# Kept output products of six of eight steps in high and low parts, four operand sets, and half of layer two's weight sums by accumulating DMAs

## The chip, the cores and the metric

One Trainium2 chip, one of its cores. The time is the device time of one execution in microseconds (us); of several runs the median counts.

## What is computed

```python
qn = q / (np.linalg.norm(q, axis=1, keepdims=True) + 1e-06)
kn = k / (np.linalg.norm(k, axis=1, keepdims=True) + 1e-06)
s = kn.transpose(0, 2, 1) @ qn / tau              # 256 x 256
a = softmax(s, -1)                                # over 6016 tokens: v @ a
x = (v @ a).reshape(6016, 256)
h = x @ w_in;  x = (h * sigmoid(1.702 * h)) @ w_out       # 256 -> 2048 -> 256
h = x @ w2_in; x = np.maximum(0.01 * h, h) @ w2_out       # 256 -> 2048 -> 256
```

All arrays are float32, but the four weights, which come as 64-bit floats and are put together from their words on the chip.

## The kernel before

**Stages.** Up to about 50 us q and k are read and the attention matrix is made. Then come two layers over six token pairs each, twelve pairs in all, numbered 0 to 11 (`steps`): pairs 0 to 5 are layer one, 6 to 11 layer two. A pair is 2 x 512 tokens, the sixth pair of each layer (5 and 11) 2 x 448. A pair runs eight steps f, each with 2 x 128 hidden features. Pair 0 is the front stage (`hidden_first`), which goes on to about 146 us beside the making of the weights. Pairs 1 to 3 run `step`, which uses Strassen's scheme with seven products for the first matrix of the layer and the plain way for the second. Pairs 4 to 11 (`FIRST` = 4) run `strassen_step`, with seven products for the first matrix and seven for the second; the last two steps of pair 11 are of the other kind.

**Number format.** A product a * b is taken as three float32r matmuls, high * high, low * high and high * low (`terms`, L100). The high part is a cast (`halves`, `cast`, ACT or DVE), the low part a DVE subtraction behind it (`subtract`, through L107).

**Kept products.** The seventh output product of a step is not run in the step. Its right side, g21, is kept for all eight steps (`retained`), and the products run at the end of the pair in two bursts (`burst`, L1340), in the first step of the next pair: steps 4, 5, 0, 1 at the hook "burst", steps 2, 3, 6, 7 at the hook "join". The steps in `SPLIT` (2 to 5) are kept in high and low parts and run as three float32r matmuls, the ones in `RAW` (0, 1, 6, 7) as one float32 matmul. The high part is copied in the step, the low part is subtracted in `first_stage`, which runs near the start of step f+1.

**Operand sets.** `operands` hands out pairs of tiles in turn, three calls a step (g0, g1, g2), from five sets: four in the space of the first layer's output weights, the fifth in the two buffers with the tag "gs".

**Weights.** Layer one's sums are made by `sums_first`: `combine` sums four blocks of a weight in place by four DVE instructions, casts and lows follow, and the stores to DRAM. In the front stage `go_on(n)` runs the generator `jobs` for n yields, with the casts on DVE; what is left by then is done one piece a step, with the casts on ACT. Then `words_of` makes layer two's sixteen pieces, one a step in pairs 1 to 3: `bits` puts a piece together in a tile `ta` (two buffers), a cast of the base blocks, `second` (their low parts, the store, the sums by `combine`), a cast of the sums ("rest", L406, ACT), and `third` (their low parts and the store). Casts run in `run_casts`, in the middle of the step, `close` runs what is in `closing` behind the cast of g22, `run_due` what is in `due` at the step's end, and then `begin_next` starts a piece. The sign of the sums of w2_in is turned in some places (`minus_sum`, L113), since the second layer's input blocks are made by accumulating DMAs of GpSimd's queue (L1487), which can add but not subtract.

**What sets the order.** Each engine runs its instructions in the order in which the code is written (`manual_schedule`), and waits where data or a buffer is not there.

Of the kernel before, what the change touches and what calls it, by code (L numbers as in the profile page):

```python
# [17 lines left out]
def tile_kernel(  # L18
# [61 lines left out]
    x2 = [dram.tile([P, 4, w], F32, name=f"x2{p}") for p, w in enumerate(width)]  # L80
    raw1 = [dram.tile([P, 2, 4, P], F32, name=f"raw1{f}") for f in range(NF)]
    w2a = [dram.tile([P, 7, 2, P], F32, name=f"w2a{f}") for f in range(NF)]
    w2o = [dram.tile([P, 8, 2, P], F32, name=f"w2o{f}") for f in range(NF)]
    SPLIT = (2, 3, 4, 5)
    RAW = (0, 1, 6, 7)
    w2r = dram.tile([P, len(RAW), P], F32, name="w2r")
# [40 lines left out]
    with tc.manual_schedule():  # L127
# [28 lines left out]
        def load_piece(key):  # L156
            name, f = key
            if name == "both":
                t = raws[key] = early.tile([P, 2, 4, P], F32, tag="cv", name="cb", bufs=3)
                nc.sync.dma_start(out=t, in_=raw1[f])  # L160
                return
# [35 lines left out]

        def combine(a, turned=False):

            (minus_sum if turned else add)(a[:, 2], a[:, 3], a[:, 2])  # L200
            yield
            subtract(a[:, 3], a[:, 0], a[:, 3])
            yield
            if turned:
                minus_sum(a[:, 0], a[:, 2], a[:, 0])
            else:
                subtract(a[:, 0], a[:, 2], a[:, 0])
            yield
            subtract(a[:, 1], a[:, 1], a[:, 0])
            yield  # L210
# [48 lines left out]
        def convert(key):  # L259

            name, f = key
            if key not in scaled:
                scale_words(raws[key])
                scaled.add(key)
            yield from bits(key)
            scale_next()
            yield
            a = words_out.pop(key)
            flat = a.rearrange("p k c -> p (k c)")
            if name == "wo":  # L270
                hi, lo = (wo[f][:, s].rearrange("p k c -> p (k c)") for s in range(2))
                for j in range(2):
                    nc.sync.dma_start(
                        out=raw1[f][:, 1, 0::3] if j == 0 else raw1[f][:, 1, 1:3],
                        in_=a[:, 2 * j:2 * j + 2],
                    )
                nc.vector.tensor_copy(hi, flat)
                yield
                subtract(lo, flat, hi.bitcast(F32))
                yield  # L280
                return
            if name == "wi":
                wi = early.tile([P, 2, BLK], F32R, tag="ws", name="wi", bufs=2)
                (nc.scalar.copy if f == 0 else nc.vector.tensor_copy)(wi[:, 0], flat)
                yield
                subtract(wi[:, 1], flat, wi[:, 0].bitcast(F32))
                ready[f] = wi
                yield
                return
# [13 lines left out]
        def sums_first(f):  # L303
# [9 lines left out]

            yield from combine(t[:, 0])
            high(lambda: wa[f][:, 3:, 0], t[:, 0])
            yield from combine(t[:, 1])
            high(out_blocks, t[:, 1])

            def second():
                subtract(wa[f][:, 3:, 1], t[:, 0], wa[f][:, 3:, 0].bitcast(F32))  # L320
# [3 lines left out]
                subtract(x[:, :, 1], t[:, 1], x[:, :, 0].bitcast(F32))  # L324
                nc.sync.dma_start(out=w1o[f][:, 2:6], in_=x.bitcast(F32))
# [14 lines left out]
        def words_of(key):  # L340
# [30 lines left out]

            if name == "w2i":
                def both_bases():
                    x = kept["x"] = new_blocks(name)
                    nc.scalar.copy(x[:, 0, 0], a[:, 0])
                    nc.scalar.activation(
                        out=x[:, 1:3, 0], in_=a[:, 1:3], func=AF.Copy, scale=-1.0
                    )
                casts.append(both_bases)
            else:  # L380
                high(base_blocks, a[:, some])

            def second():
                x = kept["x"]
                if name == "w2i":
                    subtract(x[:, 0, 1], a[:, 0], x[:, 0, 0].bitcast(F32))
                    minus_sum(x[:, 1:3, 1], a[:, 1:3], x[:, 1:3, 0].bitcast(F32))
                else:
                    subtract(x[:, some, 1], a[:, some], x[:, some, 0].bitcast(F32))
                if name == "w2i":  # L390
                    nc.sync.dma_start(out=dst[:, :3], in_=x[:, :3].bitcast(F32))
                else:
# [7 lines left out]
                    else:  # L400
                        raw = early.tile([P, P], F32, tag="wr", name="wr")
                        nc.vector.tensor_copy(raw, a[:, 1])
                        nc.sync.dma_start(out=w2r[:, RAW.index(f)], in_=raw)
                for _ in combine(a, name == "w2i"):
                    pass
                casts.insert(0, lambda: nc.scalar.copy(rest_blocks(), a))  # L406
                closing.append(third)

# [7 lines left out]

            due.append(second)

# [359 lines left out]
        fold_half(raw0, 0, 1)  # L778
        nc.sync.dma_start(out=raw1[0][:, 0], in_=raw0)
        folded.add(0)  # L780
# [5 lines left out]
        def fold(f):  # L786
# [10 lines left out]
            subtract(lo, raw, hi.bitcast(F32))  # L797
            nc.sync.dma_start(out=raw1[f][:, 0], in_=raw)
            folded.add(f)
# [374 lines left out]

        sets = [(4 - 3 * (NF * (LAST - FIRST) + REST - 1)) % 5]

        def operands(name):
            i = sets[0] % 5
            sets[0] += 1
            if i == 4:  # L1180
                return [late.tile([P, 2, BLK], F32R, tag="gs", name=name, bufs=2) for _ in range(2)]
            return [
                (early if n < EARLY else late).tile([P, 2, BLK], F32R, tag=f"wo{n}", name=name)
                for n in (2 * i, 2 * i + 1)
            ]
# [3 lines left out]
        def retained(i, f):  # L1189
# [13 lines left out]
            elif n > 1:  # L1203
                t = late.tile([P, 2, BLK], F32R, tag=("cc", "gq")[n - 2], name="keep1")
                keep[i, f] = t[:, :, :w]
# [11 lines left out]
        def strassen_step(i, f):  # L1217
# [51 lines left out]
            def first_stage():  # L1269
# [47 lines left out]
        def begin_drain(i):  # L1317
# [40 lines left out]
            def part_two():  # L1358
                if i == LAST:
                    return  # L1360
                add(to["c"], to["c"], sums[i, M5])
                add(tb, ta, sums[i, M7])

            def join():
                burst(other)
                if i == LAST:
                    add(ta, ta, sums[i, M6])
                    add(tb, ta, sums[i, M7])
                    add(ta, ta, sums[i, M5])
# [62 lines left out]
        def place_v(i, n):  # L1432
            nc.vector.transpose(out=staged_x[i][:, n], in_=vblocks_in.pop(n))

        def cast(to, i, n, j):
            nc.scalar.copy(to[:, 0, n, :width[i % NPAIR]], staged_x[i][:, j])

        def low(to, i, n, j):
            w = width[i % NPAIR]
            subtract(to[:, 1, n, :w], staged_x[i][:, j], to[:, 0, n, :w].bitcast(F32))  # L1440

# [218 lines left out]
```

## Time and profile before

| | us |
|---|---|
| median of 3 runs (1005.89 to 1007.33) | 1006.01 |
| profiled execution | 1006.63 |
| its span, first to last instruction | 1004.9 |
| PE busy | 997.7 (99%) |
| DVE busy | 881.5 (88%) |
| ACT busy | 760.8 (76%) |
| GpSimd (POOL) busy | 21.8 (2%) |

PE is TensorE's matmuls, DVE VectorE, ACT ScalarE, SP the queue of most DMAs. Matmuls are pipelined: a record of 512 columns lasts about 0.39 us, but the next one starts 0.23 us after it. So what a matmul takes on PE is read from one start to the next. A row of a timeline joins neighbours of the same kind; its time runs to the end of the last record.

### The profile page before, as it was taken

How to read it: one execution, taken by the hardware profiler on the slowest of the kernel's cores; microseconds unless marked ns; L12 is line 12 of the kernel's file. 1: busy time of each engine (PE TensorE's matmuls, PEld its weight loads, DVE VectorE, ACT ScalarE, POOL GpSimd, SP SyncE). 2: the span in 40 equal slices, each digit the busy share in tenths (PEclk: the TensorE clock that was granted, in tenths of full speed). 3: DMA queues.
4: the chain of work that ended last, by engine and by line, in shares of the span. 5: the costliest groups of instructions: out<-in, count | busy, mean ns of one | idle time of the engine just before them, and what ended most of it. 6: DMA issues, size and time to landing. Idle time of an engine off the chain costs nothing.

```text
span 1004.9 us, 13108 instructions
## 1 busy us (share of the span) xinstructions
PE 997.7 (99%) x4448; PEld 824.6 (82%) x4448; DVE 881.5 (88%) x1304; ACT 760.8 (76%) x1221; POOL 21.8 (2%) x31
## 2 busy tenths in 40 slices
PE   9999999999999999999999999999999999999998
PEld 8888887887888888877998887887887887788897
DVE  7899977878887887999898998998998998998986
ACT  7775557787878787886887886886886897797683
POOL 0000000000000000000000000000000000000000
PEclk9999999999999999999999999999999999999999
DMA  9866477745546753764976775875875875785662
GB/s 347 271 178 183 153 236 247 249 174 189 158 152 195 228 177 84 255 211 139 308 242 218 263 227 168 240 237 180 248 225 193 219 234 188 211 260 178 177 205 48
DMA packets 161619, 208.36 MB, mean 207 GB/s; under 512 B 100624, under 2 KB 126736, under 8 KB 160400
## 3 DMA queue, kind: packets, MB, share of 16 engines
q1 hardware_dynamic: 153808, 200.38, 61.4%
q0 software_dynamic: 3456, 6.16, 3.7%
q10 hardware_dynamic: 4288, 0.98, 0.5%
q8 instruction: 35, 0.57, 0.2%
q14 instruction: 32, 0.26, 0.1%
HBM read 161.87 MB, written 45.61 MB: 206 GB/s over the span
## 4 chain that ended last, share of the span: by engine, by line
PE 97%; DMA 1%; DVE 1%; issue 0%; ACT 0%; ACTq 0%; SPq 0%; DVEq 0%
PE h L100 53%; PE y L841 18%; PE y L100 17%; PE y L1340 5%; PE y L565 3%; DMA qk<-in_k_dram 1%; PE h L712 1%; PE h L841 0%; PE y L712 0%; DVE cc L107 0%; ACTq L498 0%; PE y L670 0%; DVE ta L107 0%; PE h L585 0%; DVE ta L247 0%
## 5 line engine op out<-in xcount | busy, mean ns | idle before, releaser
L100 PE MATMUL h<-xa,wi 128*128 128x512 f32 (+1 forms) x765 | 201.9, 385 | 0.0
L100 PE MATMUL y<-g,wo 128*128 128x512 f32 (+1 forms) x744 | 198.5, 389 | 0.4 <-issue 0.4
L100 PEld LDWEIGHTS h<-xa,wi 128*128 128x128 f32 x765 | 141.5, 188 | 29.7 <-ACT tv L1233 3.3
L100 PEld LDWEIGHTS y<-g,wo 128*128 128x128 f32 x744 | 139.6, 188 | 29.2 <-issue 4.5
L100 PE MATMUL h<-xb,wi 128*128 128x512 f32 (+1 forms) x573 | 152.8, 391 | 0.0
L107 DVE TENSOR_TENSOR g<-t,g 128x1024 fp32r<-128x1024 f32 (+1 forms) x124 | 147.4, 1189 | 0.0
L100 PEld LDWEIGHTS h<-xb,wi 128*128 128x128 f32 x573 | 106.9, 188 | 24.5 <-issue 3.2
L841 PE MATMUL y<-gd,wo 128*128 128x512 f32 (+1 forms) x498 | 124.2, 388 | 0.0
L841 PEld LDWEIGHTS y<-gd,wo 128*128 128x128 f32 x498 | 93.1, 188 | 18.7
L100 PE MATMUL h<-xa,wa 128*128 128x512 f32 x384 | 104.2, 390 | 0.1
L100 PE MATMUL h<-g,wo 128*128 128x512 f32 (+1 forms) x372 | 102.7, 384 | 0.0
L811 ACT ACTIVATE g<-g 128x512 f32<-128x512 f32 (+1 forms) x92 | 57.8, 628 | 44.3 <-DVE g L107 43.3
L100 PE MATMUL h<-xb,wa 128*128 128x512 f32 x312 | 83.9, 391 | 0.7 <-DVE xb L104 0.5
L100 PEld LDWEIGHTS h<-xa,wa 128*128 128x128 f32 x384 | 71.5, 188 | 15.4 <-DVE cc L107 0.5
L100 PEld LDWEIGHTS h<-g,wo 128*128 128x128 f32 x372 | 69.8, 188 | 12.7
L841 PE MATMUL y<-g,wo 128*128 128x512 f32 (+1 forms) x297 | 79.1, 388 | 0.0
L1277 ACT CAST g<-t 128x1024 fp32r<-128x1024 f32 (+1 forms) x62 | 63.8, 1029 | 19.5 <-DVE t L107 18.3
L107 DVE TENSOR_TENSOR g<-g,g 128x1024 fp32r<-128x1024 f32 (+1 forms) x62 | 73.9, 1192 | 0.3
L107 DVE TENSOR_TENSOR t<-g 128x1024 f32<-128x1024 f32 (+1 forms) x62 | 73.2, 1181 | 0.0
L100 PEld LDWEIGHTS h<-xb,wa 128*128 128x128 f32 x312 | 58.3, 188 | 14.0 <-DVE xb L104 1.0
L107 DVE TENSOR_TENSOR g<-tt,h 128x512 f32<-128x512 f32 (+1 forms) x62 | 41.7, 672 | 31.2 <-ACT tt L1241 26.9
L1248 ACT CAST g<-g 128x1024 fp32r<-128x1024 f32 (+1 forms) x62 | 63.7, 1027 | 2.0
(192 smaller groups left out, 1525.6 us busy)
## 6 DMA issues: line engine op xcount, KB each, us to landing
wi<-w2a SPq DMA_DIRECT2D x48, 896.0 KB, 5.5
wo<-w2o SPq DMA_DIRECT2D x46, 768.0 KB, 4.2
wi<-w1a SPq DMA_DIRECT2D x16, 896.0 KB, 6.3
wo<-w1o SPq DMA_DIRECT2D x16, 768.0 KB, 4.8
cv<-in_moe_w_in_dram SPq DMA_DIRECT2D x32, 256.0 KB, 3.4
w1a<-wa SPq DMA_DIRECT2D x8, 896.0 KB, 3.6
stg<-x SPq DMA_DIRECT2D x5, 1024.0 KB, 4.8
stg<-x POOLq DMA_DIRECT2D x20, 256.0 KB, 4.3
```

Of the source, the lines that this page charges most:

```text
L100: nc.tensor.matmul(dst, lhsT=w, rhs=x, start=start, stop=stop, skip_group_check=more)
L107: nc.vector.tensor_tensor(out=out, in0=in0, in1=in1, op=op)
L565: nc.tensor.matmul(s_ps[h][:, :C], lhsT=t[:, 1, r, h * P:(h + 1) * P], rhs=t[:, 0, r, :], start=(j == 0 and r == 0), stop=(j == last and r ...
L712: nc.tensor.matmul(pw, lhsT=e[:, d, c0], rhs=wi[:, x, d], start=i == 0, stop=i == len(todo) - 1)
L811: nc.scalar.activation(out=out, in_=in_, func=AF.Prelu, alpha=0.01)
L841: nc.tensor.matmul(ys[key][kc], lhsT=ws[x], rhs=y, start=first and n == 0, stop=closing or (final and n == 2), skip_group_check=closing,)
L1248: nc.scalar.copy(g0[0], g[:, 0::2])
L1277: nc.scalar.copy(g1[0], t13)
L1340: nc.tensor.matmul(sums[i, M1], lhsT=x, rhs=y, start=False, stop=True, skip_group_check=True,)
```

## The change

The six steps 2 to 7 are kept in parts (`SPLIT`), 0 and 1 raw; the tiles for 6 and 7 are the "gs" buffers, which the fifth operand set had. Four sets are left. In `combine` both matrices of a layer-one piece are summed at once (the DRAM tile raw1 is laid out anew for that). Of layer two's four sums two stay on DVE, and two become accumulating DMAs that GpSimd issues; `second` moves to `closing` and `third` to `due`. Signs that were turned in the weights of w2_in move to the second layer's input blocks (`turned`) and to the sums of g in layer two.

```diff
-    SPLIT = (2, 3, 4, 5)
-    RAW = (0, 1, 6, 7)
+    SPLIT = (2, 3, 4, 5, 6, 7)
+    RAW = (0, 1)
...
-            yield from combine(t[:, 0])
-            high(lambda: wa[f][:, 3:, 0], t[:, 0])
-            yield from combine(t[:, 1])
-            high(out_blocks, t[:, 1])
+            yield from combine(t)
+            high(lambda: wa[f][:, 3:, 0], t[:, :, 0])
+            high(out_blocks, t[:, :, 1])
...
-                for _ in combine(a, name == "w2i"):
-                    pass
-                casts.insert(0, lambda: nc.scalar.copy(rest_blocks(), a))
-                closing.append(third)
+                minus_sum(a[:, 2], a[:, 3], a[:, 2])
+                subtract(a[:, 3], a[:, 0], a[:, 3])
+                for to, n in ((0, 2), (1, 0)):
+                    nc.gpsimd.dma_start(out=a[:, to], in_=a[:, n], accum_op=ALU.add)
+                casts.insert(0, rest)
+
+            def rest():
+                nc.scalar.copy(rest_blocks(), a)
+                due.append(third)
...
-            due.append(second)
+            closing.append(second)
...
-        sets = [(4 - 3 * (NF * (LAST - FIRST) + REST - 1)) % 5]
+        sets = [0]
...
-            i = sets[0] % 5
+            i = sets[0] % 4
             sets[0] += 1
-            if i == 4:
-                return [late.tile([P, 2, BLK], F32R, tag="gs", name=name, bufs=2) for _ in range(2)]
...
-                t = late.tile([P, 2, BLK], F32R, tag=("cc", "gq")[n - 2], name="keep1")
+                tag = ("cc", "gq", "gs", "gs")[n - 2]
+                t = late.tile(
+                    [P, 2, BLK], F32R, tag=tag, name="keep1", bufs=2 if tag == "gs" else 1
+                )
...
-                subtract(t13, g[:, 1:3], g[:, 0:2])
-                nc.scalar.copy(g1[0], t13)
-                subtract(t24[:, 0], g[:, 2], t13[:, 0])
-                subtract(t24[:, 1], g21, t24[:, 0])
+                if layer == 1:
...
+                else:
+                    subtract(t13, g[:, 0:2], g[:, 1:3])
+                    nc.scalar.copy(g1[0], t13)
+                    minus_sum(t24[:, 0], t13[:, 0], g[:, 2])
+                    add(t24[:, 1], g21, t24[:, 0])
...
+        def turned(to, i, n):
+            return i >= NPAIR and (n in (B21, T4) if to is xbt else n == T2)
+
         def cast(to, i, n, j):
-            nc.scalar.copy(to[:, 0, n, :width[i % NPAIR]], staged_x[i][:, j])
+            hi, raw = to[:, 0, n, :width[i % NPAIR]], staged_x[i][:, j]
+            if turned(to, i, n):
+                nc.scalar.activation(out=hi, in_=raw, func=AF.Copy, scale=-1.0)
+            else:
+                nc.scalar.copy(hi, raw)
```

**PE, the second burst of pair 4's drain.** y is the sum in PSUM, keep the kept right sides, a_1 the weights. Before:

```order
L100 MATMUL h_4343<-xb,wi_4229 128x448 x3
L100 MATMUL y_3848<-g_4376,wo_4231 128x512 x2
L100 MATMUL y_3848<-g_4377,wo_4231 128x512
L1340 MATMUL y_3794<-keep_3931,a_1_3985 128x512 x6
L1340 MATMUL y_3794<-keep,a_1_3985 128x512 x2
L100 MATMUL h_4344<-xb,wi_4229 128x448 x3
```

And now:

```order
L100 MATMUL h_4298<-xb,wi_4177 128x448 x3
L100 MATMUL y_3798<-g_4332,wo_4179 128x512 x2
L100 MATMUL y_3798<-g_4333,wo_4179 128x512
L1335 MATMUL y_3744<-keep_3881,a_1_3935 128x512 x6
L1335 MATMUL y_3744<-keep_4208,a_1_3935 128x512 x3
L1335 MATMUL y_3744<-keep_4289,a_1_3935 128x512 x3
L100 MATMUL h_4299<-xb,wi_4177 128x448 x3
```

The two raw matmuls, steps 6 and 7, are now three and three.

**DVE, a step of pair 2 with a weight piece.** ta is the piece, w2i, w2o, w2is and w2os are tiles with high and low parts, cc and g those of the step's own work. Before:

```order
L107 TENSOR_TENSOR tt<-tt,h_2408 128x512
L107 TENSOR_TENSOR g_2451<-tp,g_2451 128x512
L107 TENSOR_TENSOR w2os<-ta,w2os 128x4x128
L107 TENSOR_TENSOR cc<-tv,h_2408 128x512
L107 TENSOR_TENSOR g_2452<-tt,g_2452 128x512
L107 TENSOR_TENSOR w2i<-ta,w2i 128x128
L113 SCALAR_TENSOR_TENSOR w2i<-ta,w2i 128x2x128
L113 SCALAR_TENSOR_TENSOR ta<-ta 128x128
L107 TENSOR_TENSOR ta<-ta 128x128
L113 SCALAR_TENSOR_TENSOR ta<-ta 128x128
L107 TENSOR_TENSOR ta<-ta 128x128
L242 TENSOR_SCALAR ta<-cv 128x512
```

And now, the step beside it:

```order
L107 TENSOR_TENSOR tt<-tt,h_2313 128x512
L107 TENSOR_TENSOR g_2359<-tp,g_2359 128x512
L107 TENSOR_TENSOR w2o<-ta,w2o 128x3x128
L113 SCALAR_TENSOR_TENSOR ta<-ta 128x128
L107 TENSOR_TENSOR ta<-ta 128x128
L107 TENSOR_TENSOR cc<-tv,h_2313 128x512
L107 TENSOR_TENSOR g_2360<-tt,g_2360 128x512
L107 TENSOR_TENSOR w2is<-ta,w2is 128x4x128
L903 STREAM_TRANSPOSE stg<-xr 128x512
L239 TENSOR_SCALAR ta<-cv 128x512
```

Two sums (ta<-ta) are gone from DVE; the low part of the base and the two sums that are left stand ahead of cc, and the low part of the rest, of the piece before, behind g.

**DVE, the front stage.** cb are layer one's pieces, wa and wt their high and low parts, gd the hidden activations of pair 0. Before:

```order
L107 TENSOR_TENSOR cb<-cb 128x128 x3
L301 CAST wa_124<-cb 128x4x128
L301 CAST wt<-cb 128x4x128
L107 TENSOR_TENSOR wa_124<-cb,wa_124 128x4x128
L107 TENSOR_TENSOR wt<-cb,wt 128x4x128
L107 TENSOR_TENSOR cb<-cb 128x128
L107 TENSOR_TENSOR gd<-h,gd 128x1024
```

And now, ahead of the same gd:

```order
L107 TENSOR_TENSOR cb<-cb 128x256
L298 CAST wa_126<-cb 128x4x128
L298 CAST wt<-cb 128x4x128
L107 TENSOR_TENSOR wa_126<-cb,wa_126 128x4x128
L107 TENSOR_TENSOR wt<-cb,wt 128x4x128
L107 TENSOR_TENSOR cb<-cb 128x256 x3
L107 TENSOR_TENSOR gd<-h,gd 128x1024
```

The gd that stood behind the second piece (wa_124) now stands behind the third (wa_126) and three sums of the fourth.

## Rows read from the trace of the kernel before

**Rows 1.** Table of stretches: us, busy us (count) of each engine, granted clock, DMA share, GB/s

```profile
core 0: us, PE busy (x) PEld busy (x) DVE busy (x) ACT busy (x) POOL busy (x), PEclk, DMA share, GB/s
50.00:150.00 100.00, 100.00 (x484) 83.99 (x483) 90.77 (x166) 58.00 (x96) 0.00 (x0) 1.00 0.62 185
...
225.00:309.00 84.00, 83.47 (x368) 68.72 (x367) 72.57 (x139) 66.90 (x121) 0.00 (x0) 1.00 0.50 166
...
687.00:765.00 78.00, 78.00 (x335) 62.37 (x334) 72.05 (x88) 62.08 (x94) 3.46 (x4) 1.00 0.72 217
```

**Rows 2.** PE's timeline, second bursts of two drains: start us, us, what, count

```profile
697.73 3.24 PE L1340 MATMUL y<-keep,a 128*128 128x512 f32 x10
...
699.10 0.59 PE L1340 MATMUL y<-keep,a 128*128 128x512 f32 x1
...
699.95 0.59 PE L1340 MATMUL y<-keep,a 128*128 128x512 f32 x1
...
543.52 2.90 PE L1340 MATMUL y<-keep,a 128*128 128x448 f32 x10
...
544.76 0.54 PE L1340 MATMUL y<-keep,a 128*128 128x448 f32 x1
...
545.51 0.54 PE L1340 MATMUL y<-keep,a 128*128 128x448 f32 x1
```

**Rows 3.** DVE's groups (count, busy us, mean ns, idle) and its timeline, step 0

```profile
L107 DVE TENSOR_TENSOR keep<-raw,keep 128x512 fp32r<-128x512 f32 x24 | 16.4, 685 | 0.0
...
692.76 0.69 DVE L107 TENSOR_TENSOR g<-tt,h 128x512 f32<-128x512 f32 x1 [1.35 <-ACT tt L1241]
```

**Rows 4.** Table of stretches, step 7 of pair 4 and of pair 7

```profile
454.81:463.58 8.77, 8.77 (x41) 7.32 (x40) 8.45 (x11) 7.47 (x12) 0.00 (x0) 1.00 0.56 192
678.45:687.29 8.84, 8.84 (x41) 7.32 (x40) 7.30 (x9) 7.56 (x12) 0.00 (x0) 1.00 0.56 190
```

**Rows 5.** Timelines of DVE, PE and ACT, a step of pair 2 with weights

```profile
264.86 0.69 DVE L107 TENSOR_TENSOR w2is<-ta,w2is 128x512 fp32r<-128x512 f32 x1
265.46 0.68 DVE L107 TENSOR_TENSOR cc<-tv,h 128x512 f32<-128x512 f32 x1
...
266.66 0.55 DVE L107 TENSOR_TENSOR w2o<-ta,w2o 128x384 fp32r<-128x384 f32 x1
267.25 1.27 DVE L107 TENSOR_TENSOR ta<-ta 128x128 f32<-128x128 f32 x4
...
266.85 0.84 PE L100 MATMUL h<-xa,wa 128*128 128x512 f32 x3
...
272.30 0.62 ACT L406 CAST w2os<-ta 128x512 fp32r<-128x512 f32 x1
```

**Rows 6.** DMA: queue's share, issues, landing of GpSimd's; timelines of DVE and GpSimd

```profile
q0 software_dynamic: 3456, 6.16, 3.7%
...
w2r<-wr SPq DMA_DIRECT2D x4, 64.0 KB, 2.1
...
DMA to landing us min/median/max: 3.6/4.3/8.4
...
596.15 0.69 DVE L107 TENSOR_TENSOR xa<-stg,xa 128x512 fp32r<-128x512 f32 x1
...
597.52 1.22 DVE L107 TENSOR_TENSOR g<-t,g 128x1024 fp32r<-128x1024 f32 x1
...
597.35 0.86 POOL L1487 DMA_DIRECT2D stg<-x  x1 [16.85 <-DVE xa L107]
```

**Rows 7.** Timelines of DVE and PE, front stage, and a group of casts

```profile
133.82 1.23 DVE L107 TENSOR_TENSOR gd<-h,gd 128x1024 fp32r<-128x1024 f32 x1 [0.38 <-ACT gd L1037]
...
137.34 2.88 PE L841 MATMUL y<-gd,wo 128*128 128x512 f32 x12
...
L301 DVE CAST wa<-cb 128x512 fp32r<-128x512 f32 x3 | 1.3, 421 | 0.0
```

**Rows 8.** Timeline of PE, first step of pair 2

```profile
229.09 0.50 PE L100 MATMUL h<-xb,wa 128*128 128x512 f32 x1 [0.53 <-DVE xb L104]
```

More of the change, by code (lines that the diff above doesn't have):

```diff
@@ L80, in tile_kernel @@
     x2 = [dram.tile([P, 4, w], F32, name=f"x2{p}") for p, w in enumerate(width)]
-    raw1 = [dram.tile([P, 2, 4, P], F32, name=f"raw1{f}") for f in range(NF)]
+    raw1 = [dram.tile([P, 4, 2, P], F32, name=f"raw1{f}") for f in range(NF)]
     w2a = [dram.tile([P, 7, 2, P], F32, name=f"w2a{f}") for f in range(NF)]
     w2o = [dram.tile([P, 8, 2, P], F32, name=f"w2o{f}") for f in range(NF)]
-    SPLIT = (2, 3, 4, 5)
-    RAW = (0, 1, 6, 7)
+    SPLIT = (2, 3, 4, 5, 6, 7)
+    RAW = (0, 1)
     w2r = dram.tile([P, len(RAW), P], F32, name="w2r")
@@ L158, in load_piece @@
             if name == "both":
-                t = raws[key] = early.tile([P, 2, 4, P], F32, tag="cv", name="cb", bufs=3)
+                t = raws[key] = early.tile([P, 4, 2, P], F32, tag="cv", name="cb", bufs=3)
                 nc.sync.dma_start(out=t, in_=raw1[f])
@@ L196, in next_load, with combine @@
                     return
-        def combine(a, turned=False):
-            (minus_sum if turned else add)(a[:, 2], a[:, 3], a[:, 2])
+        def combine(a):
+            add(a[:, 2], a[:, 3], a[:, 2])
             yield
@@ L203, in combine @@
             yield
[L204 to L207, printed above, removed]
+            subtract(a[:, 0], a[:, 2], a[:, 0])
             yield
@@ L273, in convert @@
                     nc.sync.dma_start(
-                        out=raw1[f][:, 1, 0::3] if j == 0 else raw1[f][:, 1, 1:3],
+                        out=raw1[f][:, 0::3, 1] if j == 0 else raw1[f][:, 1:3, 1],
                         in_=a[:, 2 * j:2 * j + 2],
@@ L312, in out_blocks @@
                 return kept["x"][:, :, 0]
-            yield from combine(t[:, 0])
-            high(lambda: wa[f][:, 3:, 0], t[:, 0])
-            yield from combine(t[:, 1])
-            high(out_blocks, t[:, 1])
+            yield from combine(t)
+            high(lambda: wa[f][:, 3:, 0], t[:, :, 0])
+            high(out_blocks, t[:, :, 1])
             def second():
-                subtract(wa[f][:, 3:, 1], t[:, 0], wa[f][:, 3:, 0].bitcast(F32))
+                subtract(wa[f][:, 3:, 1], t[:, :, 0], wa[f][:, 3:, 0].bitcast(F32))
                 combined.add(f)
@@ L323, in second @@
                 x = kept["x"]
-                subtract(x[:, :, 1], t[:, 1], x[:, :, 0].bitcast(F32))
+                subtract(x[:, :, 1], t[:, :, 1], x[:, :, 0].bitcast(F32))
                 nc.sync.dma_start(out=w1o[f][:, 2:6], in_=x.bitcast(F32))
@@ L370, in rest_blocks @@
                 return kept["y"][:, :, 0]
[L372 to L381, printed above, removed]
+            high(base_blocks, a[:, some])
             def second():
                 x = kept["x"]
[L385 to L389, printed above, removed]
+                subtract(x[:, some, 1], a[:, some], x[:, some, 0].bitcast(F32))
                 if name == "w2i":
@@ L778, in tile_kernel @@
         fold_half(raw0, 0, 1)
-        nc.sync.dma_start(out=raw1[0][:, 0], in_=raw0)
+        nc.sync.dma_start(out=raw1[0][:, :, 0], in_=raw0)
         folded.add(0)
@@ L797, in fold @@
             subtract(lo, raw, hi.bitcast(F32))
-            nc.sync.dma_start(out=raw1[f][:, 0], in_=raw)
+            nc.sync.dma_start(out=raw1[f][:, :, 0], in_=raw)
             folded.add(f)
@@ L1275, in first_stage @@
                 hook("first")
-                subtract(t13, g[:, 1:3], g[:, 0:2])
-                nc.scalar.copy(g1[0], t13)
-                subtract(t24[:, 0], g[:, 2], t13[:, 0])
-                subtract(t24[:, 1], g21, t24[:, 0])
+                if layer == 1:
+                    subtract(t13, g[:, 1:3], g[:, 0:2])
+                    nc.scalar.copy(g1[0], t13)
+                    subtract(t24[:, 0], g[:, 2], t13[:, 0])
+                    subtract(t24[:, 1], g21, t24[:, 0])
+                else:
+                    subtract(t13, g[:, 0:2], g[:, 1:3])
+                    nc.scalar.copy(g1[0], t13)
+                    minus_sum(t24[:, 0], t13[:, 0], g[:, 2])
+                    add(t24[:, 1], g21, t24[:, 0])
                 subtract(g1[1], t13, g1[0].bitcast(F32))
@@ L1361, in part_two @@
                 add(to["c"], to["c"], sums[i, M5])
-                add(tb, ta, sums[i, M7])
+                (add if layer == 1 else subtract)(tb, ta, sums[i, M7])
             def join():
@@ L1367, in join @@
                     add(ta, ta, sums[i, M6])
-                    add(tb, ta, sums[i, M7])
+                    subtract(tb, ta, sums[i, M7])
                     add(ta, ta, sums[i, M5])
@@ L1433, in place_v @@
             nc.vector.transpose(out=staged_x[i][:, n], in_=vblocks_in.pop(n))
+        def turned(to, i, n):
+            return i >= NPAIR and (n in (B21, T4) if to is xbt else n == T2)
         def cast(to, i, n, j):
-            nc.scalar.copy(to[:, 0, n, :width[i % NPAIR]], staged_x[i][:, j])
+            hi, raw = to[:, 0, n, :width[i % NPAIR]], staged_x[i][:, j]
[3 more added lines that the diff above has]
+                nc.scalar.copy(hi, raw)
         def low(to, i, n, j):
             w = width[i % NPAIR]
-            subtract(to[:, 1, n, :w], staged_x[i][:, j], to[:, 0, n, :w].bitcast(F32))
+            hi, lo = (to[:, x, n, :w] for x in range(2))
+            (minus_sum if turned(to, i, n) else subtract)(lo, staged_x[i][:, j], hi.bitcast(F32))
         def between(i, f):
```

## Prediction

> **What bounds the kernel now.** I read the table of stretches first, for the share of each engine, then the timelines of PE and DVE where the diff works. TensorE is busy for over 99% of each stretch [rows 1] at a granted clock of 1.00, the higher of its two levels (2.4 GHz): the kernel ends when PE's columns are through, and a change pays only where it takes columns from PE or a wait off it. Behind PE stands DVE: 90.77 of 100 us in the front stage and 72.05 of 78 in a pair of layer two [rows 1], 8.45 of 8.77 in a step of pair 4 [rows 4]. ACT has more air (62.08 of 78). So each piece of new DVE work has to be asked where it lies, and each piece taken off DVE is worth nothing unless PE waited for it.
>
> **The kept products, the part that PE sees.** A kept product in raw float32 is one product that the trace shows as two records. In a burst of ten records the first six (two products in high and low parts) start at 697.73 and end where the raw ones begin, at 699.10: 1.37 us, 0.228 each. The first raw product runs from 699.10 to the next at 699.95: 0.85 us [rows 2]. In three parts it would take 3 x 0.228 = 0.685, so a product saves 0.165 us. In the pair of 448 columns: 543.52 to 544.76 is 1.24 for six, 0.62 for three; 544.76 to 545.51 is 0.75; it saves 0.13 [rows 2]. Steps 6 and 7 change from raw to parts. They are kept in pairs 4 to 10, seven pairs, of which pair 5 has 448 columns; the last pair keeps steps 0 to 5 alone and gains nothing. 12 x 0.165 + 2 x 0.13 = **2.2 us off PE**, all in the second burst of each drain, on the path.
>
> What it adds: per product one ACT copy into the high part and one DVE subtraction of 0.685 us (keep<-raw,keep [rows 3]), 14 of each. The subtraction of step f runs in the first stage of step f+1. So the new ones run in step 7 and in step 0 of the next pair. In step 7 DVE is busy for 7.30 of 8.84 us [rows 4]; in step 0 it stood idle for 1.35 us ahead of 692.76, waiting for ACT [rows 3], just behind the place where the new one goes, and the burst that reads it starts at 697.73 [rows 2]. Both fit. In pair 4 there is no such gap: DVE is busy 8.45 of the 8.77 us of its step 7 [rows 4]. 8.45 + 0.69 = 9.14, 0.3 over PE's step of 8.84: **0.3 us back** (0 to 0.7; the gap of step 0 takes up the rest). ACT's copies lie in the two steps that have had none so far; nothing for them.
>
> Four operand sets for five: a set comes back after four calls, that is when the first stage of step f+2 writes it, and what it held was read by PE in step f+1; only the second column of a t24 is read later, in step f+2, and its set is the one that the second half of that step writes. Nobody waits: nothing, and if I have this wrong it is a wait of ACT's cast in every step of pairs 4 to 11. The turned signs swap one DVE or ACT form for another of the same size: nothing.
>
> **The front stage.** The sums of layer one are done in four instructions of 256 elements a piece where there were eight of 128, and the generator yields after each, so the same calls get further: five pieces lie ahead of step (1,0) where there were three. DVE has 9 us of idle time in the stage [rows 1], but late. Ahead of the subtraction at 133.82 (the first that found DVE idle, for 0.38 us [rows 7]) now stand one whole piece more (four sums at about 0.42, two casts at 0.42, two lows at 0.69: 3.9; a 256-wide sum lies between 0.29 and 0.69, taken like the cast of 0.42 [rows 5, 7]) and two to three more sums (1.0), less two pieces' saving of 0.6 each (8 x 0.29 less 4 x 0.42): 3.7, and 3.3 after the idle 0.38. It would end at 133.82 + 3.3 + 1.23 = 138.3. PE's block that reads it starts at 137.34 and reads the low part in its third product, 0.45 later [rows 7], at 137.8: **0.5 us** lost once (0 to 1.2). Behind it DVE catches up: the stretch has 9 us of idle time, and little of it lies ahead of that place.
>
> **Layer two's weight sums.** Sixteen pieces, one a step, in pairs 1 to 3. Of four sums of 128 elements two go from DVE to GpSimd's queue as accumulating DMAs. DVE loses two times 0.32 us a step (1.27 us for four [rows 5]); PE was waiting for DVE there once, 0.53 us for the three xb lows at 229.09 [rows 8], and this wait should go: **0.5 us gained**. What the new order may cost:
> - The first two sums and the base's low part now stand ahead of cc<-tv,h, where the rest's low part (0.68) stood. Base low 0.59 (from its start at 266.66 to the sums at 267.25) and two sums 0.64 make 1.23 for 0.60 (264.86 to 265.46): cc moves from 265.46 to 266.09 and ends at 266.77. PE's next step overwrites what it reads at 266.85 [rows 5]. The cover shrinks from 0.7 to 0.1 us, but holds.
> - ACT's cast of the rest now waits for both DMAs, one after the other since each reads what the other wrote. Behind it on ACT stand the scaling, the base's cast, and the g11 cast that DVE waits for, then cc, then PE. The sums end at 264.86 + 0.59 + 0.64 = 266.09, and the next rest cast starts at 272.30 [rows 5]: **a window of 6.2 us**, 6.3 with the cover.
> - The chain: GpSimd started its DMA at 597.35, 0.51 after the DVE instruction that released it (596.15 + 0.69) [rows 6], so 0.51 stands ahead of each. No row has a 64 KB DMA of that queue. From above: 256 KB took 4.3 in the middle and 3.6 at least to land. From below: 64 KB on SP's queue, 2.1 [rows 6]. So two steps take between 5.2 and 9.6. Nearest is the same queue with fewer bytes: 3.7% of 16 engines' span over 24 DMAs is 1004.9 x 0.037 / 24 = 1.55 us a DMA; a quarter of the bytes saves 1.15. That gives 2.45 to 3.15, the chain 5.9 to 7.3. I take the lower end, since the DMA engines were busy for 0.72 of the time where the 24 ran and are for 0.50 in pair 2 [rows 1]; **the chain fits with 0.3 to spare**. In pair 3 the first weight streams share the engines with four pieces; for them and odd others 0.3 us in all.
>
> **Sum**: -2.2 + 0.3 + 0.5 - 0.5 + 0.3 = -1.6. The profiled execution took 1006.63, 0.6 over the median of 1006.01; so 1005.0 in its terms, **1004.4 us** for the median. On the forecast alone: without any of the costs 1003.3, and 1002.9 if the median falls 0.4 off; with each at its upper end (0.7, 1.2, the wait at 229 kept, 0.6 for the chain) 1006.3.
>
> **Rivals.**
> - *The sums' chain is late where other transfers run* (pair 3, four pieces, and those beside loads of v): 0.3 to 1.2 us a piece on six to eight pieces, 2 to 7 us: 1006 to 1011. For: the 24 DMAs of the same queue spread from 3.6 to 8.4 [rows 6]. Against: those that took longest ran beside streams that pairs 1 and 2 don't have.
> - *The chain is late in every piece*, the slower side. From 6.3 us on ACT's wait goes one for one to PE: ACT stands, DVE's low of g11 stands, cc comes after PE's overwrite is due. At the 7.3 worked out above it costs 1.0 x 16 = 16: 1020; at 6.8 half of that, 1012. For: the window is 6.2 and the middle row alone would break it. Against: bytes and load are lower.
> - *DVE is full in layer two*: the two lows push PE although they stand at the gaps, because DVE has 72.05 + 1.4 of 77.7 us. Then the 0.3 us of pair 4 comes back in each of seven pairs, 2.1: 1006.5. For: six of eight steps have no gap. Against: rows 3, the gaps stand exactly where the work goes.
> - *GpSimd is shut out by DVE.* GpSimd's issue at 597.35 ran beside a two-input subtraction of DVE's (597.52 [rows 6]), and I found none of the 24 beside a copy or another one-input instruction. In the new order the two issues stand near the raw copy and the one-input shift of the next piece's words. If each has to wait out one such instruction, a cast's 0.42 [rows 7], the chain is 5.9 + 0.84 = 6.7, 0.4 over in each piece, 0.4 x 16 = 6: 1011. The Trainium skill, "SBUF — State Buffer", section "SBUF: two separate sides", says this: DVE in a two-port mode locks GpSimd out and it cannot write descriptors. By that rule the time could be 1011; the trace leaves it open.
>
> **How the numbers follow.** Forecast (the chain hidden) 0.64: it ends faster by over 0.2% (2.0 us, about what a measurement of this kernel can tell from no change) when the front stage or pair 4 cost less than I put, 0.34, and within it otherwise, 0.30. Late in places 0.14: same 0.08, slower 0.06. Late everywhere 0.09: slower. Full DVE 0.08: same 0.07, slower 0.01. Shut out 0.05: slower 0.04, same 0.01. Together faster 0.34, same 0.46, slower 0.20. The range goes from the forecast's lower end, 1002.9, through full DVE and most of late in places to 1009.5; it leaves out the chain late everywhere, shut out and the last of late in places, 0.16.
>
> **What would show it.** Right: in the second burst twelve records of 0.228 us instead of ten; no gap of PE in pairs 1 to 3 and none at 229; ACT's rest cast right behind the tt copy; DVE's gaps in steps 7 and 0 down by 0.6. Wrong: rest casts released by a DMA, DVE's wait for the g11 cast longer by as much, steps of pairs 1 to 3 longer than before; PE waiting for a gd low part near 137.8 for over 1 us; PE waiting for g adds in step 7 or 0 of layer two. The prediction falls if two DMAs take over 6.3 us from the sums to the cast.

## The result and the profile after

The changed kernel took 1017.92 us (median of 4 runs, 1016.92 to 1020.12) where the kernel before, run beside it, took 1006.16. The ratio is 1.0116, with a 95% interval of 1.0103 to 1.0128: slower, and outside the range of 1002.9 to 1009.5. The profiled execution of the changed kernel took 1017.69, its span 1015.9.

Where the time went is seen by cutting both spans at the first step of pair 1 and at that of pair 4. These are the tables of stretches of the kernel before and of the changed one, from the start of pair 1 to that of pair 4 and from there to the end: us, busy us (count) of each engine, granted clock, DMA share, GB/s.

```profile
146.38:390.37 243.99, 243.20 (x1070) 200.04 (x1069) 200.89 (x380) 189.09 (x332) 0.00 (x0) 1.00 0.59 192
390.37:1004.90 614.53, 609.55 (x2685) 500.80 (x2683) 553.13 (x685) 479.62 (x731) 20.91 (x24) 1.00 0.67 208
```

```profile
146.65:403.24 256.59, 246.54 (x1069) 200.49 (x1069) 185.41 (x306) 186.88 (x321) 27.68 (x32) 0.99 0.62 181
403.24:1015.90 612.66, 607.41 (x2699) 503.07 (x2697) 560.33 (x699) 487.15 (x745) 20.73 (x24) 1.00 0.68 208
```

The front stage ends 0.27 us later, which the first step gives back. From pair 4 on the kernel is 1.87 us faster. Pairs 1 to 3, where layer two's weight sums are made, are 12.60 us slower, although DVE works 15.5 us less there. PE's waits name the cause at their end (the waits of PE in the changed kernel: what waited, for what, us in all, times, longest):

```profile
PE h L100 <- DVE cc L107: 9.4, 5, 2.7
PE y L829 <- DVE gd L107: 0.2, 1, 0.2
```

The lost time stands in single steps ((p,f) is step f of pair p). Most steps of pairs 1 to 3 take 10.20 us as before; longer are (2,1) by 3.5, (2,2) by 1.1, (2,4) by 2.5, (2,7) by 0.5, (3,2) to (3,4) by 1.8, 2.0 and 1.6, (1,6) and (1,7) by 0.6 together; (2,0) is 0.8 shorter, since the wait of [rows 8] is gone. Step (2,1) on the timeline of all engines (start us, us, engine, line, what, idle time before it and its releaser):

```profile
235.80 0.86 POOL L390 DMA_DIRECT2D ta<-ta  x1 [7.35 <-ACT cc L797]
...
238.33 0.32 SPq L868 DMA_DIRECT2D x<-stg  x1
238.40 0.86 POOL L390 DMA_DIRECT2D ta<-ta  x1 [1.74 <-DVE stg L862]
...
244.52 0.62 ACT L394 CAST w2is<-ta 128x512 fp32r<-128x512 f32 x1 [2.87 <-DMA ta<-ta]
245.05 0.65 ACT L212 ACTIVATE cv<-cv 128x512 f32<-128x512 f32 x1
245.60 0.50 ACT L298 CAST w2o<-ta 128x384 fp32r<-128x384 f32 x1
246.00 0.62 ACT L1127 CAST g<-tp 128x512 fp32r<-128x512 f32 x1
...
246.65 0.69 DVE L107 TENSOR_TENSOR g<-tp,g 128x512 fp32r<-128x512 f32 x1 [4.16 <-ACT g L1127]
...
248.38 0.68 DVE L107 TENSOR_TENSOR cc<-tv,h 128x512 f32<-128x512 f32 x1
...
249.12 1.53 PE L100 MATMUL h<-xa,wa 128*128 128x512 f32 x3 [2.65 <-DVE cc L107]
```

This is the chain that the prediction wrote down, link by link: the second DMA lands late, ACT's cast of the rest (L394) waits 2.87 us for it, behind it stand the scaling, the base's cast and the g11 cast (L1127), DVE stands 4.16 us for that, cc comes late, PE stands 2.65. A step where it fits, (2,3):

```profile
259.95 0.29 DVE L107 TENSOR_TENSOR ta<-ta 128x128 f32<-128x128 f32 x1
...
260.77 0.86 POOL L390 DMA_DIRECT2D ta<-ta  x1 [8.30 <-ACT cc L797]
...
266.52 0.62 ACT L394 CAST w2is<-ta 128x512 fp32r<-128x512 f32 x1
```

What differs is the time that the second DMA takes to land. The view of one tile gives it for the DMAs issued from 260 to 264, for the one at 238.40, and for the six from 345 to 376 (pair 3):

```profile
DMA to landing us min/median/max: 2.3/2.3/2.4
...
DMA to landing us min/median/max: 6.1/6.1/6.1
...
DMA to landing us min/median/max: 2.3/3.7/4.9
```

From the sums' end to the second landing a quiet chain takes 0.53 + 2.33 + 0.28 + 2.33 = 5.5 us, less than the 5.9 forecast. The late ones take 6.6 and 6.8 (one each in pairs 1 and 2), 8.1 to 8.3 (four in pair 3), 8.8 in (2,4) and 9.2 in (2,1). What ran beside the DMA at 238.40 shows the DMA table of 238.3 to 245 (queue: packets, MB, share of 16 engines; issues with KB and us to landing):

```profile
q1 hardware_dynamic: 780, 1.93, 77.5%
q0 software_dynamic: 144, 0.07, 11.6%
q8 instruction: 1, 0.02, 1.3%
...
x<-stg SPq DMA_DIRECT2D x1, 1024.0 KB, 5.9
cv<-in_moe_w_in_dram SPq DMA_DIRECT2D x2, 256.0 KB, 5.1
ta<-ta POOLq DMA_DIRECT2D x1, 64.0 KB, 6.1
```

The store of pair 1's result was issued 0.07 us ahead of the sum; its 128 records of 8 KB run from 239.23 to 243.79. A quiet sum's first record starts 1.43 us after the issue; this one's starts after 3.47, at 241.87, when 122 of the store's 128 records have started. The other six, the rest of one DMA engine's share of eight, come one after the other: a record of 16 KB of instructions (queue q8) had run from 239.51 for 1.45 us. Of the sum's own 128 records 120 were through at 242.91; the last eight stood behind the last of the store's and ended at 244.17. So of the 3.7 us that this DMA was late some 2.0 go with the store, some 0.4 with what ran among its records (loads of words), and some 1.3 with the instruction record.

In pair 3 the neighbours of the late second DMAs are the weight streams (896 and 768 KB), but not in (3,2): the stream nearest to it was issued at 340.91, behind both of its DMAs (334.91 and 339.38). Its first DMA met a record of 16 KB of instructions at 336.13 (0.96 us), its second the loads of v issued from 338.62.

### The profile page after: what moved, and what is told of

The parts are those of the page before. It is cut to its first block, busy times and chain, and to the rows that moved or that the text cites. A ratio compares the mean times of both kernels' runs of the same rounds, so it can differ in the third digit from the quotient of the medians.

```text
span 1015.9 us, 13137 instructions
## 1 busy us (share of the span) xinstructions
PE 999.6 (98%) x4462; PEld 827.5 (81%) x4462; DVE 878.5 (86%) x1248; ACT 765.6 (75%) x1223; POOL 49.2 (5%) x63
## 4 chain that ended last, share of the span: by engine, by line
PE 62%; DVE 1%; DMA 0%; issue 0%; ACT 0%; ACTq 0%
PE h L100 39%; PE y L100 16%; PE y L1335 4%; PE y L829 3%; DMA ta<-ta 0%; DVE g L107 0%; PE h L829 0%; DVE t L107 0%; DVE o L1406 0%; ACT g L1272 0%; DVE w2o L107 0%; DVE cc L107 0%; DVE xa L107 0%; ACT w2o L298 0%; ACT g L1127 0%
## 5 line engine op out<-in xcount | busy, mean ns | idle before, releaser
L100 PEld LDWEIGHTS y<-g,wo 128*128 128x128 f32 x744 | 139.5, 188 | 29.3 <-issue 4.5
L100 PE MATMUL h<-xb,wi 128*128 128x512 f32 (+1 forms) x573 | 150.2, 386 | 0.3 <-DVE g L107 0.2
L829 PEld LDWEIGHTS y<-g,wo 128*128 128x128 f32 x297 | 56.6, 191 | 12.0
```

The lines of the kernel that those rows point to most:

```text
L100: nc.tensor.matmul(dst, lhsT=w, rhs=x, start=start, stop=stop, skip_group_check=more)
L829: nc.tensor.matmul(ys[key][kc], lhsT=ws[x], rhs=y, start=first and n == 0, stop=closing or (final and n == 2), skip_group_check=closing,)
```

## The experiments

Two theories. **Chain**: the 12.6 us are the two DMAs, late beside large transfers, and ACT's order passes the delay on. **Order**: the new places of the base's low part and the sums ahead of cc cost it, whoever makes the sums. The results together (pairs 1 to 3 and pair 4 to the end are from each kernel's profiled execution):

```
kernel                        median us   ratio to before [95%]     pairs 1-3   pair 4 to end
before                        1006.2-1007.0                            244.0      614.5
changed                       1017.92     1.0116 [1.0103, 1.0128]      256.6      612.7
e1 sums on DVE                1005.54     0.9991 [0.9982, 1.0000]      244.7      612.8
e2 one DMA                    1013.67     1.0069 [1.0056, 1.0082]      251.8      613.0
e3 rest cast later            1003.75     0.9975 [0.9965, 0.9985]      242.9      612.3
e4 kept products alone        1005.67     0.9992 [0.9983, 1.0001]      244.1      613.1
e5 store behind               1013.29     1.0068 [1.0054, 1.0082]      251.4      613.0
e6 streams, moved in text     1016.29     1.0102 [1.0086, 1.0118]      255.3      612.7
e7 e5 and e6                  1014.70     1.0074 [1.0055, 1.0093]      250.3      612.4
e8 DMA sums alone, cast later 1005.91     0.9995 [0.9986, 1.0004]      242.9      614.4
e9 streams behind             1011.71     1.0049 [1.0034, 1.0064]      252.6      612.5
e10 e5 and e9                 1009.34     1.0023 [1.0014, 1.0033]      249.5      613.1
e11 plain copies (one run)    1012.41                                  250.4      613.2
```

**e1: the DMAs undone.** In place of the DMAs (`due.append(more_sums)`, so behind cc):

```
-                for to, n in ((0, 2), (1, 0)):
-                    nc.gpsimd.dma_start(out=a[:, to], in_=a[:, n], accum_op=ALU.add)
+                    add(a[:, to], a[:, to], a[:, n])
```

> The changed kernel with its accumulating DMAs alone undone: the third and fourth sum are DVE additions again, placed behind cc in the same step, so that nothing new stands ahead of cc; order of the rest, kept products and operand sets as changed. Theory 'chain' (the 12.9 us lost in pairs 2 and 3 are waits for the two DMAs): all steps of pairs 1 to 3 at 10.2 again, 1006.2 - 1.85 (gained from pair 4 on) = 1004.3, up to 1004.8 if the wait of 0.5 at 229 comes back. Theory 'order' (base low and two sums ahead of cc, or the rest cast ahead of the scaling on ACT, cost it whoever makes the sums): steps of pairs 2 and 3 stay long, 1010 or more.

Measured 1005.54; no step waits for cc any more. So Chain holds for some 11.9 of the 12.6 us. The time lies 0.7 over the forecast's upper end, and pairs 1 to 3 are 0.7 longer than before: that is the order's part. (1,6), (1,7) and (2,7) are as long as in the changed kernel, and (3,2) is 0.2 longer than in the kernel before. At the end of pair 2, in e1:

```profile
306.96 0.68 DVE L107 TENSOR_TENSOR cc<-tv,h 128x512 f32<-128x512 f32 x1
...
307.67 0.63 ACT L800 ACTIVATE cc<-cc 128x512 f32<-128x512 f32 x1 [0.80 <-DVE cc L107]
...
308.21 1.65 ACT L103 CAST xb<-stg 128x512 fp32r<-128x512 f32 x3
...
309.76 0.58 ACT L1109 COPY h<-h 128x512 f32<-128x512 f32 x1
...
310.39 0.97 PE L100 MATMUL h<-xa,wa 128*128 128x512 f32 x3 [0.31 <-ACT h L1109]
```

cc comes later behind the base's low part and the sums, ACT waits 0.80 us for it (0.27 in the kernel before), and here alone three xb casts and then the h copy that PE needs stand behind.

**e2: one DMA for two.** As e1, but the fourth sum by a DMA behind the third (`add(a[:, 0], ...)`, then `nc.gpsimd.dma_start(out=a[:, 1], in_=a[:, 0], accum_op=ALU.add)`).

> Half of the chain: the third sum by DVE behind cc, the fourth alone by an accumulating DMA (16 DMAs for 32, none waiting for another). Theory 'chain': the DMA is issued some 2 us later than the first was, and 0.53 + 2.33 for a quiet one give 4.9 us from the first sums to the cast, under the 6.3 from which ACT's wait reaches PE; a DMA that takes as long as the slow ones did (3.3 to 6.06) overshoots by 0 to 2.3. So 1004.3 with no slow one, up to 1008.5 with all. Theory 'each DMA costs something by itself' (a fixed loss per DMA, 12.9 / 32 = 0.4): 16 x 0.4 over 1004.3, 1010.7. Theory 'order': 1010 or more.

Measured 1013.67, 5 over the upper end of theory chain; by the sum alone the rival "each DMA costs" is nearer, and order's "1010 or more" holds. Order had fallen with e1. Against a cost of each DMA the trace decides: 13 of the 16 DMAs cost PE nothing, and three steps lose 2.8, 2.9 and 1.8 us, (2,1), (3,3) and (3,4). The view of the tile ta, all 16 DMAs:

```profile
DMA to landing us min/median/max: 2.3/2.7/6.6
```

The expectation took over the landing times of the changed kernel. But a DMA issued 2 to 3 us later meets what runs then: at 344.32 it stood 0.27 us behind a stream of 896 KB and landed after 6.56. A shorter chain is no safer if it starts at a worse place.

**e3: both DMAs kept, ACT's cast of the rest moved** behind the g22 cast:

```
-                casts.insert(0, rest)
+                rests.append(rest)
...
             nc.scalar.copy(g22[:, 0], tt)
+            run_rests()
```

> Both DMAs as in the changed kernel, at the same place; moved is only ACT's cast of the rest, from the head of its step's casts to behind the g22 cast, four ACT instructions or some 2.6 us later. Theory 'chain late beside other transfers': the DMAs are as slow as before in some pieces (4 to 6 us), but only the slowest chain (9.2) still overshoots, by 0.3: 1004.0 to 1004.8. Theory 'order' or 'the DMAs themselves disturb DVE, GpSimd or SP': the DMAs are all still there, so 1010 or more.

Measured 1003.75, ratio 0.9975: faster than both kernels, and 0.25 under the expected range. The DMAs are as slow as before: eight land after 3.4 to 6.4 us, where ten took 3.3 to 6.1 in the changed kernel. PE waits for none of them. The view of the tile ta, then ACT in step (2,1):

```profile
DMA to landing us min/median/max: 2.3/2.4/6.4
```

```profile
243.87 0.62 ACT L1135 CAST g<-tt 128x512 fp32r<-128x512 f32 x1
244.51 0.62 ACT L394 CAST w2is<-ta 128x512 fp32r<-128x512 f32 x1
```

The second DMA landed at 244.45; every step of pair 2 from (2,1) to (2,6) takes 10.20. The order's loss is gone too: the base's cast moves up on ACT, the base's low part and the sums on DVE with it, and cc stands at its old place.

**e4: the kept products and operand sets alone**, in the kernel before (`SPLIT = (2, 3, 4, 5, 6, 7)`, `RAW = (0, 1)`, sets by `% 4`).

> The kernel before with the first two parts of the change alone: six kept products in parts and four operand sets; layer one's sums, layer two's sums and the signs as before. The prediction's own terms: -2.2 on PE, +0.3 in pair 4, so 1004.3; the trace of the changed kernel gave -1.85 from pair 4 on, so 1004.3 as well. Theory 'DVE is full in layer two': 1006 or more.

Measured 1005.67, a gain of 0.7 with an interval from 1.7 to none; its profiled execution is 1.4 us faster from pair 4 on. The measured time lies between the expected 1004.3, a gain of 2.1 that is outside the interval, and the 1006 of the rival. The trace has a part of the difference: PE lost 0.3 at 424, waiting for DVE in pair 4, which the changed kernel did not.

**e5: the store of pair 1 behind the second DMA**, `nc.gpsimd` for `nc.sync` at L868 for p = 1.

> The changed kernel with one transfer moved: the 1 MB store of pair 1's result (x<-stg), issued in step (2,1) on SP's queue 0.07 us ahead of the second accumulating DMA of a piece, goes to GpSimd's queue, behind that DMA. All else as changed. Theory 'chain late beside other transfers' with the store as the neighbour in (2,1): that DMA lands in 2.3 to 3 us instead of 6.06, PE's wait of 2.65 at 249 and the half clock of 3.4 us behind it go, steps (2,1) and (2,2) fall from 13.7 and 11.3 to 10.2: 1017.9 - 4.6 = 1013.3 (1012.8 to 1014.0), the other late steps unchanged. Theory 'the loads of the words (cv) that start at 240 hold it': the DMA stays at 4 us or more and (2,1) stays over 11.5.

Measured 1013.29, the 1013.3 worked out, but the agreement to a tenth is luck. The step (2,1) takes 10.71 and (2,2) 10.20, 0.5 short of the whole gain. And the other late steps did not stay as they were: (3,2) lost 0.2 for 1.8, (3,3) 3.7 for 2.0 with a half clock of its own, (3,4) 0.6 for 1.6, though no stream was moved. The DMA in (2,1) lands in 3.6 us, neither the 2.3 to 3 of the theory nor the 4 of its rival. Its first record is in time, 1.43 us after the issue; the last eight end some 0.9 us late, beside an instruction record of 1.41 us. The DMA table of e5 from 238.8 to 244:

```profile
q8 instruction: 1, 0.02, 1.7%
...
ta<-ta POOLq DMA_DIRECT2D x1, 64.0 KB, 3.6
```

So the store was one of two causes in (2,1), and the larger.

**e6 and e7: the streams called half a step later in the program**, alone and with e5's move.

> The changed kernel with the six weight streams of pair 3 (wi<-w1a, wo<-w1o; 896 and 768 KB) issued half a step later, behind the rest cast, that is after both accumulating DMAs of a piece have landed and before those of the next are issued. All else as changed. Theory 'late beside the streams': the three PE waits of 1.3 to 1.7 in steps (3,2) to (3,4) go, 1017.9 - 5 = 1012.9 (1012.3 to 1013.8), steps (2,1), (2,2), (2,4) unchanged. Theory 'pair 3 is late from the loads of v or of its own': the waits stay, 1017 or more.

> Both moves together, accumulating DMAs and rest cast as in the changed kernel. If the two causes are apart from each other, the gains add: 1017.9 - 4.6 - 5 = 1008.3 (1007.5 to 1009.5); what stays over the kernel without DMA sums is step (2,4), 2.5, where an instruction load held one engine, and some 1.1 at the ends of pairs 1 and 2. If lateness only moves to the next neighbour, 1011 or more.

e6 measured 1016.29: not the 1012.9 expected, but no evidence for the rival either. SP issued the streams at the same place as before, 0.43 us behind the rest's store, for a stream on SP's queue waits for its slot alone. Even so (3,2) lost 0.2 for 1.8, while (3,3) lost 3.7 with a half clock behind it. e7 measured 1014.70 (four runs from 1011.21 to 1016.32, the fastest of them profiled); it is e5 with the same miss, and no second test of the streams.

**e9 and e10: the streams really behind the DMAs**, by GpSimd's queue (`stream_in(..., nc.gpsimd)`), alone and with e5's move.

> The changed kernel with the six weight streams of pair 3 on GpSimd's queue, where they stand behind both accumulating DMAs of their step. (In e6 they kept their time: on SP's queue a stream waits for its slot alone, not for its place in the program; it was issued 0.43 us behind the rest's store in both, 349.20 in the changed kernel and 346.51 in e6.) Theory 'late beside the streams': the accumulating DMAs of steps (3,2) to (3,5) take 2.3 to 3 us in place of 3.3 to 4.9, the waits of PE of 1.3 to 1.7 go, 1017.9 - 5 = 1012.9 (1012 to 1014). Theory 'pair 3 is late from something else' (loads of v, the 512 KB stores): waits of 1 us or more stay in two or three steps, 1016 or more.

> The streams as in e9 and pair 1's store as in e5, all else as changed. If the causes are apart and add: 1013.3 - 5 = 1008.3 (1007.3 to 1009.5), with waits of PE left in step (2,4) and 0.2 to 0.5 in (2,1). If lateness moves to the next neighbour: 1011 or more.

e9 measured 1011.71, 0.3 under its range: the waits of pair 3 are gone, and its DMAs from 345 on land like this:

```profile
DMA to landing us min/median/max: 2.3/2.4/2.8
```

For (3,3) and (3,4) that is the streams. (3,2) is no evidence for them: no stream stood ahead of its DMAs, and in e5, e6 and e7, with the streams where they were, it had lost no more than 0.2 either.

e10 measured 1009.34, in the range of causes that add. The gains as measured, 4.6 in e5 and 6.2 in e9, would make 1007.1; the 2.3 that are missing are no more than the four intervals allow. What is left is mostly (2,4), 2.9 us, and 1.1 in the step behind it at half clock. Neither stream nor 1 MB store ran there. In the changed kernel its first DMA's records started in time, but the last came 1.2 us late, beside a record of 16 KB of instructions that ran for 1.51 us; in e10 one of 1.55 us stands there. The DMA table of the changed kernel from 271 to 275:

```profile
q8 instruction: 1, 0.02, 2.4%
q14 instruction: 1, 0.01, 0.9%
...
ta<-ta POOLq DMA_DIRECT2D x1, 64.0 KB, 3.9
```

So the second started late as well, and met the loads of the next words.

**e8: the DMA sums with the later cast, without the kept products.**

> The accumulating DMAs with ACT's cast of the rest behind the g22 cast, and the rest of the change, but the kept products and the operand sets as in the kernel before (four in parts, four raw, five sets). If the parts add: the kernel with both gave 1003.75 and its steps from pair 4 on gained 2.2, so 1005.9 less what is noise of the front stage, 1005.3 to 1006.0; the wait of 0.5 at 229 gone, its step 0.7 shorter. If the DMA sums also serve pair 4 on (DVE), under 1005.

Measured 1005.91, in the expected range. Pairs 1 to 3 are 1.1 us faster than before, 0.7 of it in step (2,0), the rest at 614.4: so in the profiles the parts add. The medians alone don't show it: e4 gains 0.7 and e8 0.6, e3 with both 2.6, and each interval is about 0.9 to either side. Nor is the 1 us of pairs 1 to 3 the DMAs' alone: the moved cast brings the g11 cast forward too, and no run has the moved cast with all sums on DVE.

**e11: plain copies for the accumulating DMAs** (the two sums are left out).

> The changed kernel with plain copies in place of the accumulating DMAs, same queue, same bytes, same place (the two sums are left out, so layer two's weights are others). If the accumulation is a part of what a DMA takes, the quiet ones land in under 2.2 us in place of 2.33 and the slow ones shrink with them; if the queue and the neighbours set it, 2.3 again, 4 to 6 in the same steps, 1017 or so.

One run measured 1012.41, some 5 under the 1017 of the second theory. GpSimd's issue takes 0.53 us for 0.86, and the landings are

```profile
DMA to landing us min/median/max: 1.8/2.2/6.0
```

So accumulation is a part of a quiet DMA, and the slow ones are slow without it: ten take over 3 us, 3.1 to 6.0, as ten of the changed kernel take 3.3 to 6.1. PE loses less here than in the changed kernel: a quiet chain takes 4.8 us for 5.5, and the clock stayed at 1.00.

## Why the prediction was wrong, step by step

**The step that failed** is the chain of layer two's sums: "the chain fits with 0.3 to spare. In pair 3 the first weight streams share the engines with four pieces; for them and odd others 0.3 us in all". The quiet chain was shorter than forecast. Eight of the sixteen chains were 1.1 to 3.7 us longer than a quiet one, and the part of the loss that goes with the DMAs (e1) is 11.9 us. The window itself was right: steps lose what a chain takes over 6.3 us, to within 0.6, as (2,4) shows with 8.8 - 6.3 = 2.5, and by the chain ACT, DVE, PE that was named. (The last piece has no scaling and no base's cast behind it on ACT, and lost 0.1 by a chain of 8.2.)

**Why it was sized wrong.** [rows 6] held the answer: landings from 3.6 to 8.4, a tail of 4 us over the middle. The estimate used the mean and the lower end, and priced the tail at 0.3 to 1.2 us a piece in the rival "late where other transfers run". That rival is what happened, at 12 us where its price was 2 to 7 (its own bounds, 1.2 us on eight pieces, make 9.6), and only in part in its places: pair 3 lost 5.4, and (2,1), (2,2) and (2,4), which it did not name, 7.1. The worst neighbour, pair 1's store of 1 MB, was not looked for, nor were the records of 16 KB of instructions, which held back the last records of four of the eight late chains. Both could have been listed from the kernel before: there the store was issued at 239.32 (238.33 now), and instruction records ran at 238.84 and 267.99 (239.51 and 272.29 now). The argument against it, "those that took longest ran beside streams that pairs 1 and 2 don't have", overlooked that store. The Trainium skill, "DMA: Bandwidth & Descriptors", section "Queues, rings and completion order", says that each DMA engine takes turns between the queues, but drains a whole packet of one, 9 to 17 descriptors as a rule, before it goes to the next. The trace agrees: the store gives each of 16 engines 8 records of 8 KB, most of 0.31 to 0.37 us, and the sum's first record came 2.64 us after the store's first, when all engines but one had started their eight.

**cc's cover.** "The cover shrinks from 0.7 to 0.1 us, but holds" is right for PE in the quiet steps, and wrong at the ends of pairs 1 and 2, where ACT too waits for cc and has the xb casts behind it (e1): 1.1 us, and 0.2 more in (3,2).

**The wait at 229** went, as forecast: 0.5 of wait, and 0.7 to 0.8 of step (2,0).

**The kept products.** Twelve records, as forecast, in the burst of the changed kernel that answers [rows 2], 2.72 us to the next instruction:

```profile
710.05 2.88 PE L1335 MATMUL y<-keep,a 128*128 128x512 f32 x12
712.77 0.84 PE L100 MATMUL h<-xb,wi 128*128 128x512 f32 x3
```

The two terms, -2.2 and +0.3, make -1.9 from pair 4 on; measured were 1.9 in the changed kernel and 1.3 to 2.2 in the others with them. In pair 4 step 7 takes 9.20 us for 8.77, and step 6 no longer than before (458.33 to 467.39, for 445.45 to 454.55): 0.4 back where 0.3 was forecast. These rows are that step and step 7 of pair 7, which answer [rows 4]:

```profile
467.94:477.14 9.20, 9.16 (x41) 7.28 (x40) 8.99 (x12) 7.97 (x13) 0.00 (x0) 1.00 0.54 184
691.06:699.93 8.87, 8.87 (x41) 7.31 (x40) 7.90 (x11) 8.11 (x13) 0.00 (x0) 1.00 0.65 199
```

In step 7 of pair 7 DVE is busy for 0.60 us more, and the step takes 8.87 us for 8.84; the gap of DVE in step 0 shrank from 1.35 [rows 3] to 0.75:

```profile
705.11 0.69 DVE L107 TENSOR_TENSOR g<-tt,h 128x512 f32<-128x512 f32 x1 [0.75 <-ACT tt L1230]
```

So both lows stand at the gaps, and "DVE is full in layer two" falls, apart from pair 4.

**The front stage** waits where it was said to, for gd's low part, 0.2 us for 0.5, and the first step of pair 1 gives it back:

```profile
137.65 1.65 PE L829 MATMUL y<-gd,wo 128*128 128x512 f32 x6 [0.21 <-DVE gd L107]
```

**GpSimd shut out.** In the changed kernel every issue but the first takes 0.86 or 0.87 us. In e2 twelve issues stand beside DVE's shift, a one-input instruction, and ten of them take 0.86 or 0.87 too, so the rival gives nothing to count. The rule of the Trainium skill that it drew on ("SBUF — State Buffer", "SBUF: two separate sides") was not seen to cost time here; an issue beside a copy came once, in e2 at 238.46, and took 1.09, 0.23 more, with two other one-input instructions beside it. One case decides nothing.

**What stays open.** e4's gain is known only to 1 us. What the instruction records cost was read from traces; no run moved them. How much of e3's gain over the kernel before is the DMAs' and how much the new place of the cast was not tried apart.

## What to carry to other kernels

A DMA that stands in a chain between two engines is sized by its tail, not by its middle: list the large transfers and the loads of instructions that can stand ahead of it at that place, and take the landing beside the worst. If the slack doesn't cover that, move the consumer in its own engine's order first (four ACT instructions later turned a loss of 1.2% into a gain of 0.25% here); a shorter chain or moved neighbours brought less. A DMA's place in the program is not its place in time: it goes out when its own queue and its own wait allow.

## What the hardware showed unasked

After some of the long waits PE came back at its lower level. In the changed kernel, behind the wait of 2.65 us that ended at 249.12 (us, busy us of each engine, granted clock, DMA share, GB/s):

```profile
249.00:250.50 1.50, 1.38 (x4) 1.10 (x5) 1.50 (x4) 0.63 (x1) 0.85 (x1) 0.59 0.69 220
250.50:252.50 2.00, 2.00 (x6) 1.59 (x5) 1.93 (x4) 1.53 (x2) 0.86 (x1) 0.50 0.90 291
```

The granted clock is 0.50 (1.2 GHz) for 3.41 us; that is the 1.1 us that (2,2) lost, though its own chain was in time. The clock fell in the same way at a wait of 2.53 in e5, of 2.67 and 2.88 in e6, of 2.40 and 2.08 in e9 and of 2.09 in e10; behind waits of 2.22 in the changed kernel and of 2.51 and 2.56 in e2 the clock stayed at 1.00. So (2,1) and (2,2) lost 4.6 us for a wait of 2.65, and the runs here don't say behind which waits it happens.
